# Sparse attention and an ELU layer on one core: more of the attention output transposed by DMA

## The chip, the cores and the metric

The kernel runs on one core of one Trainium2 chip. The metric is device time in microseconds (us) of one launch, lower is better. Three runs of the kernel before gave 321.51, 318.53 and 321.12 us, median 321.12.

## The reference

Eight batches of eight heads, 576 positions, 64 elements per head. Heads 0 to 3 are *local*: position i sees positions i-31 to i. Heads 4 to 7 are *strided*: i sees every earlier position with the same remainder modulo 32. Then an MLP with ELU over all 4608 tokens (512 to 2048 to 512).

```
rel = pos[:, None] - pos[None, :]
mask_local = (rel >= 0) & (rel < 32)
mask_strided = (rel >= 0) & (pos[None, :] % 32 == pos[:, None] % 32)
scores = where(mask, q @ k.T / sqrt(64), -1e9)          # per batch and head
attn = softmax(scores) @ v
x = attn.transpose(0, 2, 1, 3).reshape(8 * 576, 512)
h = x @ w_in
out = where(h > 0, h, exp(min(h, 0)) - 1) @ w_out
```

## The kernel before

**Tiles.** Two heads make a pair; a batch has two strided pairs S0, S1 and two local pairs L0, L1. A strided pair is cut into five groups of rows of like remainders, a local pair into six blocks of 96 queries. For each pair: transposed q and k (`qT`, `kT`), masked scores as probabilities `pr`, `av` (probabilities times v, with a column of ones for the sum), and `x`, the normalised result with tokens on the partitions. The MLP needs x with features on the partitions; that is `xT`, 128 features of a pair by all tokens, and making it is the step `x_out`.

**Order.** The instruction order is written by hand: there is no scheduler. After an opening for batch 0, nine stages run, one for each chunk of 512 tokens, nb = 0 to 8. Stage nb holds, in 16 steps s, the first MLP matrix of chunk nb (`moe_in`, four matmuls, L664), its ELU (`moe_act`: exp on ACT L690, then DVE L697 and L699) and the second matrix (`moe_out`, four matmuls, L713, mostly of chunk nb-1). Woven in between is the attention of batch nb+1: `attention` gives each piece of work a half step (a "gap", 0 to 31; gap 2s stands before `moe_in` of step s, gap 2s+1 behind it) from the table `TIMES`: where each pair begins, and the offsets of its pieces. In stages 1 and 2 the strided pairs come first, from stage 3 (batch `LATE` = 4) on the local ones. At about 31.5 us a stage, a gap is about 1 us.

**x_out.** For strided pairs, and for local pairs of batches 0 to 3, PE transposes the groups or blocks of `x` against an identity into PSUM (L607, L620), and ACT or DVE copies to `xT` (L614 and L616 put the strided rows in token order, L624 the local ones). Local pairs of batches 4 to 7 go by a DMA transpose that SP issues (L599), straight from `x` into `xT`.

**Loads and queues.** POOL issues all loads of a batch, strided q, k, v, then local q, k, v, three batches ahead (`load_batch`), each with a cast to bf16 into `nat`, which has three buffers for each of q and k. From batch 3 on, q and k are transposed by DMA (`transpose_batch`, issued on SP: L226 strided, one transfer each for q and k; L234 local, two each). SP also issues the stores of the result (L720). Each engine's queue runs in order: an instruction that waits holds back those behind it.

When `transpose_batch` was called before: for batch 3 at step 6 (strided) and 13 (local) of stage 1; for batch 4 at step 6 of stage 2, strided then local; for batches 5 to 7 at step 9 of stages 3 to 5, local then strided.

Of the kernel before, what the change touches and what calls it, by code (L numbers as in the profile page):

```python
# [14 lines left out]
ACT = mybir.ActivationFunctionType  # L15
# [14 lines left out]
C_ORDER = (2, 3, 0, 1)  # L30


PIECES = (-2, -1, 0, 2, 3, 5, 7, 0)
TIMES = (
    None,
    None,
    ((4, 10, 15, 21), 0, (-3, -2, 0, 2, 4, 6, 9, 2)),
    ((2, 9, 15, 22), 0, (-2, -1, 0, 2, 3, 5, 8, 0)),
    ((2, 8, 15, 22), 0, PIECES),
)  # L40


# [23 lines left out]
def kernel(  # L66
# [66 lines left out]
    def bf16_bank():  # L133
        return rings["ring"].next().bitcast(BF16)
# [17 lines left out]
    def several(n, name, *shape):  # L152
        return [consts.tile([128, *shape], BF16, tag=f"{name}{i}", name=f"{name}{i}")
                for i in range(n)]

    nat = {(n, kind): several(3, f"{n}_{kind}", w * D)
           for n in "qk" for kind, w in (("str", 20), ("loc", 4 * L_RUN))}

# [10 lines left out]
    BY_DMA = 3  # L171

    WHOLE = 2

    FAR = 1
    RAW = 1
# [42 lines left out]
                out=t[0:64, a, 4],  # L219
                in_=src[name][b, 2 * a:2 * a + 2, 512:576].rearrange("h p d -> p h d"))  # L220

    def transpose_batch(b, local):

        def strided():
            for name, to in (("q", qT), ("k", kT)):
                nc.sync.dma_start_transpose(out=to["str"][b % 2],  # L226
                                            in_=nat[name, "str"][b % 3])

        if BY_DMA <= b <= LATE and local < 2:
            strided()  # L230
        if b >= EARLY and local:
            for name, to, o in (("q", qT, 0), ("k", kT, 32)):
                for a in range(2):
                    nc.sync.dma_start_transpose(  # L234
                        out=to["loc"][b % 2][:, a, o:o + 640].rearrange(
                            "p (i r) -> p i r", r=128),
                        in_=nat[name, "loc"][b % 3][:, 640 * a:640 * a + 640])
        if b > LATE:
            strided()

    def load_batch(b):
        for name in "qkv":
# [20 lines left out]
    def clear_v(i, engine=nc.vector):  # L263
# [8 lines left out]
             for n in "q"}  # L272
# [2 lines left out]
    nc.scalar.activation(warm, ones[0:1, 0:1], ACT.Exp)  # L275
    nc.scalar.activation(rden.rearrange("p b s h r g -> p (b s h r g)"),
                         ones.to_broadcast([128, B * 48]), ACT.Copy)
    clear_nat(0)
    for i in range(2):
        nc.vector.memset(kT["str"][i][:, :, 126:128], 0.0)  # L280
# [70 lines left out]
    class Pair:  # L351
# [200 lines left out]
        def av(self, u):  # L552
            blocks = self.blocks(u)
            nk, nq = blocks[0][4:]
            b0 = blocks[0][1]
            n = len(blocks) // 2
            av = rings["ring"].next()[:, 0:6 * (D + 1)].rearrange(
                "q (p g d) -> q p g d", p=2, g=3)
            apart = self.strided and self.b == RAW
            vt = raw[RAW] if apart else (v_str if self.strided else v_loc)[self.b % 3]  # L560
            for p, blk, bank, i, _, _ in blocks:

                if self.b >= WHOLE:
# [5 lines left out]
                nc.tensor.matmul(to[:, 0:D] if apart else to, lhsT=pr[0:nk, o:o + m],  # L569
                                 rhs=vt[0:nk, 2 * self.hp + p, blk, :],  # L570
                                 start=True, stop=True)
# [13 lines left out]

        def step(self, what):
# [5 lines left out]
            else:  # L592
                getattr(self, {"x": "x_out"}.get(what, what))()

        def x_out(self):
# [7 lines left out]
            xt = bf16_bank()  # L603
            if self.strided:
                for g in range(5):
                    n = G_ROWS[g]
                    nc.tensor.transpose(  # L607
                        xt[:, 126 * g:126 * g + n],
                        self.x[0:n, g].rearrange("q p d -> q (p d)"),
                        identity[0:n, 0:n])  # L610
                rows = dst.rearrange("d (t r) -> d t r", r=STRIDE)
                groups = xt[:, 0:630].rearrange("d (g q) -> d g q", g=5)
# [22 lines left out]
    def attention(b, start, pitch, at):  # L635

        gaps = {}
        pairs = [Pair(b, s, hp) for s in (b < LATE, b >= LATE) for hp in range(2)]
        begin = [start + pitch * i for i in range(4)] if pitch else start
        if b >= LATE:  # L640
            gaps[begin[0]] = [pairs[3].halo]
        for i, pr in enumerate(pairs):
            for off, piece in ((at[0], pr.t_q), (at[1], pr.t_k),
                               (at[7], lambda pr=pr: pr.v_in(0)),
                               (at[7] + (b > 1), lambda pr=pr: pr.v_in(1)),
                               (at[2], lambda pr=pr: pr.scores(0)),
                               (at[3] if b < WHOLE else at[2] + (b < LATE),
                                lambda pr=pr: pr.scores(1)),
                               (at[4], lambda pr=pr: pr.av(0)),
                               (at[5] - (b >= LATE and i == 0),  # L650
                                lambda pr=pr: pr.av(1)),
                               (at[6] + (b > 1 and pr.strided) + (b >= LATE), pr.x_out), (at[5] - 2, pr.halo if b < LATE else lambda: None)):
                gaps.setdefault(begin[i] + off, []).append(piece)
        return gaps


# [145 lines left out]
    for nb in range(n_chunks + 1):  # L802
# [199 lines left out]
```

## Time and profile before

The profiled execution took 318.57 us, of which 316.8 are the span from the first to the last instruction. TensorE's granted clock was 0.996 in the mean.

| stretch | us | DVE busy | ACT busy | POOL busy | DMA share | PE instructions |
|---|---|---|---|---|---|---|
| chunk 1 (52.0 to 87.4) | 35.4 | 27.80 | 23.35 | 31.48 | 1.35 | 308 |
| chunk 2 (87.4 to 119.3) | 31.9 | 28.19 | 17.58 | 22.89 | 1.60 | 240 |
| chunk 3 (119.3 to 150.7) | 31.4 | 27.38 | 17.36 | 26.42 | 1.55 | 227 |
| chunk 4 (150.7 to 182.4) | 31.7 | 27.13 | 17.81 | 22.27 | 1.56 | 227 |
| chunk 5 (182.4 to 213.9) | 31.5 | 26.54 | 17.72 | 1.20 | 0.77 | 228 |
| chunk 6 (213.9 to 245.3) | 31.4 | 26.43 | 17.62 | 0.00 | 0.14 | 227 |

A row is one stage; the busy columns are us of each engine in it. A DMA share above 1 means that transfers overlap on the DMA engines. In the opening (to about 30 us) PE has gaps; from chunk 1 on it has next to none. How to read lines of the profile: L607 is line 607 of the kernel; PE is TensorE's matmul side, DVE is VectorE, ACT ScalarE, POOL GpSimd, SP SyncE, and a q behind a name (SPq) its queue, which issues DMAs. `single<-identity,x_s` is output <- inputs, and x5 the number of instructions merged into the line. The columns of a timeline are start, duration, engine, line, operation; a bracket gives the idle time before it and what ended that.

### The profile page before, as it was taken

The numbers are of one execution on the slowest core, as the hardware profiler recorded it, in microseconds if no ns is written. First come the engines' busy times: TensorE is split into PE (matmuls) and PEld (weight loads), VectorE is DVE, ScalarE is ACT, GpSimd is POOL, SyncE is SP. The second block draws the span as 40 slices with busy tenths as digits, with TensorE's granted clock in tenths as the row PEclk, the third lists the DMA queues.
The fourth block names the chain that finished last, engine by engine and source line by source line (L and its number), as shares of the span: only waits on it lengthen the run. The fifth ranks groups of instructions, "written<-read, shape, count | busy, mean of one in ns | idle before, by whom it ended". The sixth has DMA issues, their size and how long they took to land.

```text
span 316.8 us, 6114 instructions
## 1 busy us (share of the span) xinstructions
PE 299.8 (95%) x2240; PEld 149.1 (47%) x2240; DVE 242.6 (77%) x544; ACT 172.9 (55%) x335; POOL 137.5 (43%) x213
## 2 busy tenths in 40 slices
PE   1778989999999999999999999999999999999994
PEld 0454545545444554445444544454445444444443
DVE  7787797887889998987898788878897666766610
ACT  3577886777355645565546555655565444343411
POOL 9859526959959859958585810000000000000000
PEclk9999999999999999999999999999999999999998
DMA  6999999999999999999999992580210000101012
GB/s 108 163 179 157 167 207 126 156 124 183 139 125 167 157 187 138 99 163 154 177 163 117 163 175 61 88 156 35 68 35 35 34 33 35 66 34 36 33 68 73
DMA packets 108970, 36.33 MB, mean 115 GB/s; under 512 B 87357, under 2 KB 104453, under 8 KB 108933
## 3 DMA queue, kind: packets, MB, share of 16 engines
q0 software_dynamic: 71632, 18.10, 65.0%
q1 hardware_dynamic: 37301, 17.77, 29.1%
q8 instruction: 19, 0.31, 0.4%
q14 instruction: 18, 0.15, 0.1%
HBM read 36.70 MB, written 9.44 MB: 146 GB/s over the span
## 4 chain that ended last, share of the span: by engine, by line
PE 84%; DMA 6%; DVE 3%; POOL 2%; ACT 2%; issue 1%; POOLq 0%; ACTq 0%
PE single L713 39%; PE half L664 28%; PE single L664 9%; PE single L569 3%; DMA q_str<-in_q_dram 3%; PE pair_a L479 2%; DMA v_raw<-in_v_dram 2%; DMA k_str<-in_k_dram 2%; PE single L607 1%; ACT e_sb L690 1%; POOL k_str L191 1%; PE single L397 1%; DVE g_sb L699 1%; PE single L383 1%; DVE x_l L580 1%
## 5 line engine op out<-in xcount | busy, mean ns | idle before, releaser
L713 PE MATMUL single<-w_out_sb,g_sb 128*128 128x512 bf16 (+1 forms) x592 | 145.9, 373 | 0.0
L664 PE MATMUL half<-xT,w_in_sb 128*128 128x512 bf16 x436 | 112.6, 379 | 0.9 <-DVE g_sb L699 0.9
L690 ACT ACTIVATE e_sb<-half 128x512 f32<-128x512 f32 x109 | 65.3, 600 | 70.9 <-PE half L664 67.9
L697 DVE TENSOR_SCALAR e_sb<-e_sb 128x512 bf16<-128x512 f32 x140 | 62.5, 446 | 34.9 <-ACT e_sb L690 34.4
L713 PEld LDWEIGHTS <-g_sb 128*128 128x128 bf16 x592 | 54.8, 98 | 56.6
L664 PEld LDWEIGHTS <-w_in_sb 128*128 128x128 bf16 x576 | 52.4, 98 | 57.0 <-issue 1.3
L699 DVE TENSOR_TENSOR g_sb<-e_sb,half 128x512 bf16<-128x512 bf16 x106 | 72.9, 688 | 3.7
L664 PE MATMUL single<-xT,w_in_sb 128*128 128x512 bf16 x140 | 36.5, 379 | 0.0
L690 ACT ACTIVATE e_sb<-single 128x512 f32<-128x512 f32 x35 | 21.1, 602 | 24.4 <-PE single L664 22.3
L718 ACT COPY o_sb<-single 128x512 f32<-128x512 f32 (+1 forms) x37 | 21.2, 574 | 17.5 <-PE single L713 16.7
L485 ACT ACTIVATE pr<-pair_a 126x936 bf16<-126x936 f32 (+1 forms) x24 | 23.1, 961 | 12.4 <-PE single L479 11.9
L569 PEld LDWEIGHTS <-pr 128*128 128x128 bf16 (+3 forms) x352 | 20.0, 101 | 13.7 <-issue 1.3
L699 DVE TENSOR_TENSOR g_sb<-e_sb,single 128x512 bf16<-128x512 bf16 x34 | 23.4, 688 | 1.2
L191 POOL DMA_DIRECT2D k_str<-in_k_dram x32 | 21.1, 698 | 6.8 <-issue 2.6
L191 POOL DMA_DIRECT2D v_raw<-in_v_dram x32 | 20.7, 683 | 5.0 <-DVE v_str L436 3.7
L191 POOL DMA_DIRECT2D q_str<-in_q_dram x28 | 17.4, 641 | 4.1 <-DMA w_out_sb<-in_moe_w_out_dram 2.3
L580 DVE TENSOR_TENSOR x_l<-single,rden 96x384 bf16<-96x384 f32 x32 | 17.7, 554 | 1.1
L580 DVE TENSOR_TENSOR x_s<-single,rden 126x256 bf16<-126x256 f32 (+1 forms) x32 | 15.7, 491 | 1.1
L214 POOL DMA_DIRECT2D k_loc<-in_k_dram x20 | 15.3, 795 | 2.5 <-issue 1.5
L214 POOL DMA_DIRECT2D q_loc<-in_q_dram x20 | 15.8, 813 | 0.7 <-DMA k_str<-in_k_dram 0.7
L579 DVE RECIPROCAL rden<-single 96x6 f32<-96x6 f32 (+2 forms) x64 | 11.8, 185 | 2.0 <-PE single L569 1.6
L569 PE MATMUL single<-v_loc,pr 128*128 128x65 bf16 x192 | 11.6, 195 | 0.8 <-ACT v_loc L444 0.3
(115 smaller groups left out, 249.6 us busy)
## 6 DMA issues: line engine op xcount, KB each, us to landing
out_dram<-o_sb SPq DMA_DIRECT2D x35, 256.0 KB, 3.6
v_loc<-in_v_dram POOLq DMA_DIRECT2D x8, 288.0 KB, 8.2
k_str<-in_k_dram POOLq DMA_DIRECT2D x32, 67.5 KB, 5.0
v_raw<-in_v_dram POOLq DMA_DIRECT2D x32, 67.5 KB, 4.8
w_in_sb<-in_moe_w_in_dram POOLq DMA_DIRECT2D x4, 512.0 KB, 8.2
w_out_sb<-in_moe_w_out_dram POOLq DMA_DIRECT2D x4, 512.0 KB, 13.6
q_str<-in_q_dram POOLq DMA_DIRECT2D x28, 67.5 KB, 7.5
q_loc<-in_q_dram POOLq DMA_DIRECT2D x20, 64.0 KB, 5.2
```

The source lines that it names most:

```text
L191: engine.dma_start(out=t[0:108, h].rearrange("p g d -> p (g d)"), in_=rows[h, :, 0:30, :].rearrange("t (r g) d -> t r (g d)", g=5))
L214: nc.gpsimd.dma_start(out=t[:, h // 2, 0:4, h % 2], in_=src[name][b, h, 0:512].rearrange("(i p) d -> p i d", p=128))
L485: nc.scalar.activation(both, sc[0:nk, :, 0:w], ACT.Exp, scale=scale)
L569: nc.tensor.matmul(to[:, 0:D] if apart else to, lhsT=pr[0:nk, o:o + m], rhs=vt[0:nk, 2 * self.hp + p, blk, :], start=True, stop=True)
L579: nc.vector.reciprocal(r, av[0:nq, :, 0:n, D])
L580: nc.vector.tensor_tensor(self.x[0:nq, b0:b0 + n].rearrange("q g p d -> q p g d"), av[0:nq, :, 0:n, 0:D], r.unsqueeze(3).to_broadcast([nq, ...
L664: nc.tensor.matmul(hps, lhsT=w_in_sb[:, c, m * 128:(m + 1) * 128], rhs=xT[:, c, nb * N_TILE:(nb + 1) * N_TILE], start=start, stop=stop)
L690: nc.scalar.activation(e_sb, hps, ACT.Exp)
L697: nc.vector.tensor_scalar(e1_sb, e_sb, scalar1=1.0, scalar2=1.0, op0=ALU.min, op1=ALU.subtract)
L699: nc.vector.tensor_tensor(g_of[nb][:, m, :], e1_sb, hps, op=ALU.max)
L713: nc.tensor.matmul(ops, lhsT=g_of[nb][:, m, kk * 128:(kk + 1) * 128], rhs=w_out_sb[:, m, cols], start=(m == 0), stop=(m == MC - 1))
L718: nc.scalar.copy(o_sb, ops)
```

## The change

Strided `x` of batches 2 to 7 (the third to the last), and local `x` of the first pair of batches 2 and 3, no longer go through PE. `x_s` becomes two fixed buffers, one for each pair of a batch; ACT fills their last 32 partitions once at the start. A new piece `x_dma`, one gap after `av(1)`, has SP issue a DMA transpose of `x_s` into free space: the part of `nat["q", "str"]` of the same batch, whose q was already transposed. `x_out`, three gaps later than before (at most gap 31), copies from there to `xT` on ACT, by the same two copies. For the local pair SP issues the transpose straight into `xT`, as for later batches.

`transpose_batch` is split, and a table `TURNS` gives the steps: for batch 3 local 13, strided q and k 9; for batch 4 local 6, strided 8; for batches 5 to 7 local 8, strided q 11, strided k 14. In stages 3 to 6 the two strided pairs begin one and two gaps earlier.

With this the order on SP in stage 2 is: `x_s` of S0 (gap 8), a store, the four local transposes of batch 4 (step 6), `x_s` of S1 (gap 15), strided q and k of batch 4 (step 8), a store, `x_l` of L0 (gap 23). In stages 3 and 4: `x_l` of L0, the four local transposes, `x_l` of L1, a store, `x_s` of S0, strided q, a store, `x_s` of S1, strided k, a store.

```diff
+TURNS = ((13, 9, 9), (6, 8, 8), (8, 11, 14))
 TIMES = (
...
-    ((2, 8, 15, 22), 0, PIECES),
+    ((2, 8, 14, 20), 0, PIECES),
 )
...
+    x_str = several(2, "x_s", 6, 2, D)
...
+    X_DMA = 2
+    X_ONE = 2
+    X_WAIT = 3
...
-    def transpose_batch(b, local):
-
-        def strided():
-            for name, to in (("q", qT), ("k", kT)):
-                nc.sync.dma_start_transpose(out=to["str"][b % 2],
-                                            in_=nat[name, "str"][b % 3])
-
-        if BY_DMA <= b <= LATE and local < 2:
-            strided()
-        if b >= EARLY and local:
-            for name, to, o in (("q", qT, 0), ("k", kT, 32)):
...
-        if b > LATE:
-            strided()
+    def transpose_batch(b, s):
+
+        for what, at in zip(("loc", "str q", "str k"), TURNS[min(b - EARLY, 2)]):
+            if s != at:
+                continue
+            if what == "loc":
+                for name, to, o in (("q", qT, 0), ("k", kT, 32)):
...
+            else:
+                name = what[-1]
+                nc.sync.dma_start_transpose(out=(qT if name == "q" else kT)["str"][b % 2],
                                             in_=nat[name, "str"][b % 3])
...
+    for i in range(2):
+        nc.scalar.activation(x_str[i][96:128].rearrange("q g p d -> q (g p d)"),
+                             ones[96:128].to_broadcast([32, 12 * D]), ACT.Copy)
...
-            if self.x is None:
+            if self.strided:
+                self.x = x_str[self.hp]
+            elif self.x is None:
...
+        def by_dma(self):
+            if self.strided:
+                return self.b >= X_DMA
+            return self.b >= LATE or self.b >= X_ONE and self.hp == 0
+
+        def x_dma(self):
+            if self.strided and self.by_dma():
+                free = nat["q", "str"][self.b % 3][:, 640 * self.hp:640 * self.hp + 640]
+                self.x_t = free.rearrange("d (g q) -> d g q", g=5)
+                nc.sync.dma_start_transpose(
+                    out=self.x_t,
+                    in_=self.x[:, 0:5].rearrange("q g p d -> q (g p d)"))
+
         def x_out(self):
...
-            if self.b >= LATE and not self.strided:
+            if self.by_dma() and not self.strided:
...
+                if self.by_dma():
+                    groups = self.x_t
+                else:
...
+                               (at[5] + 1, pr.x_dma),
+                               (at[6] + (b > 1 and pr.strided) + (b >= LATE)
+                                + X_WAIT * (pr.strided and pr.by_dma()), pr.x_out), (at[5] - 2, pr.halo if b < LATE else lambda: None)):
+                gaps.setdefault(min(begin[i] + off, 31), []).append(piece)
...
-            if s == (9 if nb + 2 > LATE else 6) and nb > 0 and nb + 2 < B:
-                transpose_batch(nb + 2, int(nb + 2 >= LATE))
-            if s == 13 and nb + 2 == EARLY:
-                transpose_batch(nb + 2, 2)
+            if nb > 0 and nb + 2 < B:
+                if s in TURNS[min(nb + 2 - EARLY, 2)]:
+                    transpose_batch(nb + 2, s)
```

More of the change, by code (lines that the diff above doesn't have):

```diff
@@ L220, in load_local @@
                 in_=src[name][b, 2 * a:2 * a + 2, 512:576].rearrange("h p d -> p h d"))
-    def transpose_batch(b, local):
-        def strided():
-            for name, to in (("q", qT), ("k", kT)):
-                nc.sync.dma_start_transpose(out=to["str"][b % 2],
-                                            in_=nat[name, "str"][b % 3])
-        if BY_DMA <= b <= LATE and local < 2:
-            strided()
-        if b >= EARLY and local:
-            for name, to, o in (("q", qT, 0), ("k", kT, 32)):
[L233 to L237, printed above, removed]
-        if b > LATE:
-            strided()
+    def transpose_batch(b, s):
[4 more added lines that the diff above has]
+                for name, to, o in (("q", qT, 0), ("k", kT, 32)):
+                    for a in range(2):
+                        nc.sync.dma_start_transpose(
+                            out=to["loc"][b % 2][:, a, o:o + 640].rearrange(
+                                "p (i r) -> p i r", r=128),
+                            in_=nat[name, "loc"][b % 3][:, 640 * a:640 * a + 640])
+            else:
+                name = what[-1]
+                nc.sync.dma_start_transpose(out=(qT if name == "q" else kT)["str"][b % 2],
+                                            in_=nat[name, "str"][b % 3])
     def load_batch(b):
@@ L593, in step @@
                 getattr(self, {"x": "x_out"}.get(what, what))()
+        def by_dma(self):
[6 more added lines that the diff above has]
+                self.x_t = free.rearrange("d (g q) -> d g q", g=5)
+                nc.sync.dma_start_transpose(
+                    out=self.x_t,
+                    in_=self.x[:, 0:5].rearrange("q g p d -> q (g p d)"))
         def x_out(self):
@@ L602, in x_out @@
                 return
-            xt = bf16_bank()
+            if not self.by_dma():
+                xt = bf16_bank()
             if self.strided:
[L605 to L610, printed above, removed]
-                rows = dst.rearrange("d (t r) -> d t r", r=STRIDE)
-                groups = xt[:, 0:630].rearrange("d (g q) -> d g q", g=5)
+                rows = dst.rearrange("d (t r) -> d t r", r=STRIDE)
+                if self.by_dma():
+                    groups = self.x_t
+                else:
+                    for g in range(5):
+                        n = G_ROWS[g]
+                        nc.tensor.transpose(
+                            xt[:, 126 * g:126 * g + n],
+                            self.x[0:n, g].rearrange("q p d -> q (p d)"),
+                            identity[0:n, 0:n])
+                    groups = xt[:, 0:630].rearrange("d (g q) -> d g q", g=5)
                 copy = self.copy("x", False)
@@ L651, in attention @@
                                 lambda pr=pr: pr.av(1)),
-                               (at[6] + (b > 1 and pr.strided) + (b >= LATE), pr.x_out), (at[5] - 2, pr.halo if b < LATE else lambda: None)):
-                gaps.setdefault(begin[i] + off, []).append(piece)
+                               (at[5] + 1, pr.x_dma),
+                               (at[6] + (b > 1 and pr.strided) + (b >= LATE)
+                                + X_WAIT * (pr.strided and pr.by_dma()), pr.x_out), (at[5] - 2, pr.halo if b < LATE else lambda: None)):
+                gaps.setdefault(min(begin[i] + off, 31), []).append(piece)
         return gaps
```

## The prediction

> **What bounds the kernel now.** I read the page's busy lines first, then the waits of TensorE, then the timelines of PE, SP, POOL and ACT around every x transpose, then the landing times of the DMA transposes. The page's summary (busy time of each engine; DMA share in 40 slices of 7.9 us):
>
> ```profile
> PE 299.8 (95%) x2240; PEld 149.1 (47%) x2240; DVE 242.6 (77%) x544; ACT 172.9 (55%) x335; POOL 137.5 (43%) x213
> DMA  6999999999999999999999992580210000101012
> ```
>
> PE is busy nearly all the span, and its waits between 54 and 300 us come out as an empty list. So in chunks 1 to 8 each us taken off PE is a us gained, as long as nothing makes PE wait. The DMA engines are at nine tenths or more until 190 us: the loads of later batches fill them.
>
> The second half of chunk 2 (nb = 2, 87.3 to 119.3 us) decides my forecast. First PE there (start us, us, instruction), then SP's queue, then POOL's loads of batch 4:
>
> ```profile
> 105.20 0.42 PE L607 MATMUL single<-identity,x_s 126*128 126x126 bf16 x5
> 105.46 0.35 PE L569 MATMUL single<-v_loc,pr 128*128 128x65 bf16 x6
> ...
> 109.39 0.39 PE L479 MATMUL pair_a<-qT_loc,kT_loc 64*128 64x96 bf16 x10
> ...
> 112.61 0.35 PE L569 MATMUL single<-v_loc,pr 128*128 128x65 bf16 x6
> ```
>
> ```profile
> 98.61 3.11 SPq L226 DMA_TRANSPOSE qT_str<-q_str  x1
> 101.94 2.44 SPq L226 DMA_TRANSPOSE kT_str<-k_str  x1
> ...
> 106.56 2.59 SPq L234 DMA_TRANSPOSE qT_loc<-q_loc  x2
> 110.26 2.58 SPq L234 DMA_TRANSPOSE kT_loc<-k_loc  x2
> ```
>
> ```profile
> 104.73 0.63 POOL L218 DMA_DIRECT2D k_loc<-in_k_dram  x1
> 106.26 0.60 POOL L218 DMA_DIRECT2D k_loc<-in_k_dram  x1 [0.90 <-DMA q_loc<-in_q_dram]
> ```
>
> The reader is to see two things. Five x transposes hold PE for 0.26 us (105.20 to 105.46). And SP's local transposes of batch 4, asked for at step 6 (about 99 us), start at 106.56 and 110.26, because their loads are the last of the batch: SP waits 2.0 us for q_loc and 1.0 us for k_loc, and the two last k_loc loads land 5.4 and 4.3 us after their issue, at 110.1 and 110.6.
>
> The last view is the landing of the x_l transposes that are there already (min, median, max over eight; 5.6 at 162 us among loads, 2.6 at 225 us with none):
>
> ```profile
> DMA to landing us min/median/max: 2.6/4.1/5.6
> ```
>
> **The change, part by part. Removed from PE:** strided x of batches 2 to 7, 12 groups of five transposes. In every one the next instruction starts 0.25 to 0.26 us after the group: 12 x 0.257 = 3.1 us. The first local pair of batches 2 and 3 goes too, two groups of six (79.27 to 79.52, 110.62 to 110.88): 0.5 us. Together 3.6 us, all on the path. With them go two copies on DVE (0.45 us each, L624), which nobody waits for.
>
> **Kept on ACT:** the copies that interleave the strided rows (L614 0.61 us, L616 0.20 us), now from SBUF. A row for a copy of that kind is L444 on ACT, SBUF to SBUF, 640 elements in 0.72 us, 1.13 ns an element against 1.12 for L614: no change. At the start ACT fills two x_s buffers, 768 elements each; L276 takes 0.50 us for 384, so 0.5 to 1.0 us each. They lie in the 3.30 us in which ACT waits for q_stage (2.65 to 5.96); without that cover they cost up to 2.0.
>
> **Added to SP:** 14 DMA transposes, 1.2 us of SP each by the rows of L599 and L234 (1.20 to 1.28). SP works in order, so each stands behind what comes before it, and ACT's copy now waits for its landing, with everything on ACT behind it: the exps of the MoE (L690) and of the next scores (L485), hence DVE's maxima and PE.
>
> **Room between issue and copy:** six half steps of about 1 us in chunks 1 and 2, six and five later. Chunk 1: x_s of pair S1 is ready at 72.0 (L580 at 71.42); SP, with only an out store ahead, can issue then. The row nearest in time is the qT_str transpose at 69.6, landing 5.7 us later: 77.7, and ACT's copy is due at half step 23, about 78. The first local pair goes to SP behind qT_str and kT_str, about 79.5, and is needed at about 87.5; kT_loc took 9.1 us there. I put 0.3 us on chunk 1, between 0 and 1.5.
>
> **Chunk 2, the main cost.** For batch 4 the local transposes now come first, at step 6, the x transpose of S1 of batch 3 stands behind them (half step 15), then qT_str and kT_str. S1's x_s is ready at 103.4 (L580 at 102.81), but SP sits in front of k_loc. Loads share the DMA engines with the transposes: until 97 us three x transposes come on top, after 98 two strided ones go away; I take the loads 1 us earlier than before, uncertain by 2. Then the second kT_loc issues at 110.6, x_s1 at 111.8, and lands 4.1 us later, at 115.9. (From both sides: 2.6 after 110.8 is 113.4; 6.9, as the kT_loc of 110.26 took, after 112.85 is 119.8.) ACT's copy is due at half step 21, about 108.4. PE goes on through the scores of L1 and two more w_in groups, then needs L1's probabilities at the row 112.61, which the shortened program reaches 1.5 us sooner, at 111.1. These come after ACT's copies (0.8), exp (0.97) and DVE's mask (0.65, L487): 2.5 us after landing with the handovers. So PE stands from 111.1 to 118.4: **7.3 us**, between 4.8 and 11.2. Then the x of L0 of batch 3 waits in SP for x_s1, qT_str (3.1) and kT_str (2.4): issue near 119, landing 123 to 126; chunk 3 now starts near 124.8, so this hides behind the first stall, and would be the next one late without it.
>
> **PE after a stall.** In the opening PE idles 3.39 us until 6.41; then five transposes take 1.01 us, later sets 0.69 to 0.85, and only from 19 us on is 0.42 the rule. PE after 7 us of idling may thus run slow at first, though the clock row shows 1.00 throughout. 0 to 2 us, I take 1.0. [...]
>
> **Chunks 3 and 4.** With the strided pairs one and two half steps earlier, S1's x is ready near 145.3 in old time; SP has to finish qT_str (3.1), then the out store of step 12 (its o_sb copy ends at 145.9), and issues near 146.4. It lands 4.1 to 6.8 us later, 150.5 to 153.2. The next chunk's first group reads it (fourth matmul, 151.4) after 0.8 us of copies: PE waits 0 to 2.6 us in each of the two chunks that still have loads beside them. I take 1.0 and 0.5. In chunks 5 and 6 transposes land in 2.6 to 4.1 us: nothing. [...]
>
> **Hidden:** the load of q_str for batch b+3 now waits for batch b's copies, with POOL's queue behind it. Copies end at about 78, 109 to 117 and 151 to 158; POOL reaches these loads at 108.2, 131.8 and 158.5. Only the last is close.
>
> **Sum:** 318.57 - 3.6 + 0.3 + 7.3 + 1.0 + 1.5 = 325.1 us against the profiled execution (span 316.8 and 1.8 around it). That one is the low end of the runs shown (318.53 to 321.51, median 321.12), so for a median I go 1 us up: 326.
>
> **Rivals.** *No new waits.* If the local loads are in by the time SP asks, or ACT's blocked copy stays covered, 3.6 us come off: 315.0, with 0 to 2.6 for where the runs lie. For it: PE waits for nothing now, and ACT is busy 55%. Against it: SP did wait for q_loc until 106.56 although it asked later than it will. 0.15.
>
> *A stall that cancels the gain.* Loads 2 us earlier or more and landing in 2.6 us: x_s1 lands at 113.4 or before, PE loses at most 4.8, with no slow start and nothing at the chunk ends: 315.0 + 4.8 = 319.8. This ends not slower; it decides from a landing of 113.4. 0.27.
>
> *The chunk ends rule.* Chunk 2 passes freely, but x_s1 is late at the ends of chunks 3 to 6: 4 x 2.6 - 3.6 = +6.8, 325.4. Against it: landing 2.6 at 225 us. 0.05.
>
> My forecast: 0.53; its own range is 321.5 to 331.
>
> **How the numbers follow.** About 1% (3.2 us) is what a measurement of this kernel can tell from no change. More than 1% faster is only the first rival, and only if almost nothing is given back: 0.15. Within 1%: 0.30, the second rival and the light end of the forecast. Slower: 0.55. The range takes in the first rival's 315 and the forecast's upper bounds, 331.
>
> **What would show it.** Right: SP's kT_loc of batch 4 near 109 to 111, the x_s transpose right behind it, ACT waiting 5 to 9 us for that DMA before L643, PE idle once before the av of L1 in chunk 2, few us elsewhere. Wrong: the local transposes issuing near 99, or PE without waits in chunk 2 although ACT waits.

## The result, and the profile after

Six runs of the changed kernel gave 332.52 to 342.35 us, median 337.55; six of the kernel before, on the same chip, 318.53 to 321.60, median 320.79. The ratio is 1.045, with a 95% interval of 1.037 to 1.053: slower, in the direction of the forecast and well beyond its 326 and its range. The profiled execution took 335.6 us, 17.0 more than the profiled one of before; its span is 333.8 and TensorE's mean granted clock 0.977 (before 0.996). Here and below, medians and ranges are of all runs of a kernel and ratios of those within 1.5% of its fastest, and the profiles of three experiments (the late batches alone, the old order in chunk 2, one strided pair on TensorE) are of runs slower than that.

The page's busy times, and rows of its 40 slices (8.3 us each):

```profile
PE 299.2 (90%) x2129; PEld 146.9 (44%) x2168; DVE 244.1 (73%) x542; ACT 180.0 (54%) x337; POOL 136.7 (41%) x213
...
PE   1879989999999449999899959998999999999994
...
PEclk9999999999999959999999978999999999999999
DMA  6999999999999999989979990556052200011012
```

The weight loads of TensorE are 72 fewer (2240 before), the 72 transposes that were moved. But TensorE is no longer busy throughout: there are two slices at 4 and one at 5 in the middle, and the clock row has dips beside or behind them. TensorE's waits from 54 to 340 us, by what ended them (total, times, longest); before, this list was empty:

```profile
PE single L579 <- DVE pr L497: 8.9, 1, 8.9
PE half L695 <- ACT xT L645: 4.8, 3, 3.0
PE single L695 <- ACT xT L645: 0.8, 1, 0.8
PE single L579 <- DVE v_str L446: 0.7, 1, 0.7
```

With small ones these are 16.4 us. The first is chunk 2. SP's timeline there, then ACT's, then PE's (start, duration, engine, line, operation; in the bracket the idle time before and its releaser):

```profile
104.81 2.60 SPq L239 DMA_TRANSPOSE qT_loc<-q_loc  x2
109.10 2.65 SPq L239 DMA_TRANSPOSE kT_loc<-k_loc  x2
111.85 1.60 SPq L616 DMA_TRANSPOSE q_str<-x_s  x1
113.50 2.96 SPq L245 DMA_TRANSPOSE qT_str<-q_str  x1
116.52 2.03 SPq L245 DMA_TRANSPOSE kT_str<-k_str  x1
...
119.27 1.31 SPq L624 DMA_TRANSPOSE xT<-x_l  x1
```

```profile
118.17 1.10 ACT L643 COPY xT<-q_str 128x540 bf16<-128x540 bf16 x1 [9.35 <-DMA q_str<-x_s]
119.17 0.22 ACT L645 COPY xT<-q_str 128x36 bf16<-128x36 bf16 x1
119.30 0.96 ACT L495 ACTIVATE pr<-pair_a 128x960 bf16<-128x960 f32 x1
```

```profile
111.08 1.03 PE L695 MATMUL half<-xT,w_in_sb 128*128 128x512 bf16 x4
121.01 0.52 PE L579 MATMUL single<-v_loc,pr 128*128 128x65 bf16 x6 [8.90 <-DVE pr L497]
121.33 1.90 PE L744 MATMUL single<-w_out_sb,g_sb 128*128 128x512 bf16 x4
123.02 1.53 PE L695 MATMUL half<-xT,w_in_sb 128*128 128x512 bf16 x4
...
124.58 1.03 PE L744 MATMUL single<-w_out_sb,g_sb 128*128 128x512 bf16 x3
```

The x transpose issues at 111.85, behind the local transposes, and lands just before 118.2, when ACT's copy can start; the exp of L1's scores stands behind that copy, and the probabilities come to PE at 121.0. After the wait four matmuls of 512 columns take 1.90 and 1.53 us, where 1.03 is the rule. The landing of the x transposes (min, median, max, from issue):

```profile
DMA to landing us min/median/max: 2.6/5.0/7.8
```

This view has the landing of only four of the twelve. The trace also records the counts of the semaphores (the counters that tell an engine that a transfer is done), sixteen for each DMA; the last of the sixteen gives the landing of all: 4.5 to 7.8 us for the eight that land while a load is under way, 2.6 to 4.2 for the four behind the last load. In chunk 2 it is 118.07, 6.2 us after the issue.

The length of each stage, from the first copy of a result tile in it (L749 on ACT, L718 before) to that in the next stage, in us:

| stage | before | after | difference | the prediction's terms |
|---|---|---|---|---|
| 1 | 35.00 | 35.57 | +0.57 | -0.5 |
| 2 | 31.96 | 41.94 | +9.98 | +7.5 |
| 3 | 31.45 | 32.49 | +1.04 | +0.5 |
| 4 | 31.67 | 35.31 | +3.64 | 0.0 |
| 5 | 31.45 | 33.70 | +2.25 | -0.5 |
| 6 | 31.46 | 31.42 | -0.04 | -0.5 |

The last column sums the prediction's gains (0.26 for five transposes, ten a stage, six more in stages 1 and 2) and losses for each stage. It foresaw where the largest loss is; it is 11 us short in all, and 6 of those lie in stages 4 and 5, at the end of chunk 4 and behind it.

### The profile page after: what moved, and what is told of

Read it like the earlier page. It is cut to its first block, busy times and chain, and to the rows that moved or that the text cites. A ratio compares the mean times of both kernels' runs of the same rounds, so it can differ in the third digit from the quotient of the medians.

```text
span 333.8 us, 5988 instructions
## 1 busy us (share of the span) xinstructions
PE 299.2 (90%) x2129; PEld 146.9 (44%) x2168; DVE 244.1 (73%) x542; ACT 180.0 (54%) x337; POOL 136.7 (41%) x213
## 4 chain that ended last, share of the span: by engine, by line
PE 59%; DMA 19%; POOL 8%; issue 5%; ACT 3%; DVE 3%; SPq 1%; ACTq 0%; POOLq 0%; DVEq 0%
PE single L744 28%; PE half L695 18%; PE single L695 8%; DMA q_str<-x_s 6%; DMA w_out_sb<-in_moe_w_out_dram 5%; DMA k_str<-in_k_dram 3%; DMA v_loc<-in_v_dram 3%; PE single L579 2%; PE pair_a L489 2%; DMA v_raw<-in_v_dram 2%; POOL v_raw L200 1%; DVE g_sb L730 1%; POOL k_str L200 1%; DMA k_loc<-in_k_dram 1%; DVE e_sb L728 1%
## 5 line engine op out<-in xcount | busy, mean ns | idle before, releaser
L728 DVE TENSOR_SCALAR e_sb<-e_sb 128x512 bf16<-128x512 f32 x140 | 64.7, 462 | 43.0 <-ACT e_sb L721 42.3
L744 PEld LDWEIGHTS <-g_sb 128*128 128x128 bf16 x592 | 55.6, 99 | 64.3 <-issue 9.2
L695 PEld LDWEIGHTS <-w_in_sb 128*128 128x128 bf16 x576 | 53.3, 99 | 60.3 <-issue 2.9
L749 ACT COPY o_sb<-single 128x512 f32<-128x512 f32 (+1 forms) x37 | 21.3, 574 | 20.4 <-PE single L744 20.0
L200 POOL DMA_DIRECT2D v_raw<-in_v_dram x32 | 20.6, 690 | 18.4 <-DVE v_str L446 17.1
L200 POOL DMA_DIRECT2D k_str<-in_k_dram x32 | 20.2, 663 | 6.0 <-issue 2.9
L643 ACT COPY xT<-q_str 128x540 bf16<-128x540 bf16 x12 | 13.4, 1119 | 15.8 <-DMA q_str<-x_s 13.4
L579 PE MATMUL single<-v_loc,pr 128*128 128x65 bf16 x192 | 11.9, 197 | 10.4 <-DVE pr L497 8.9
L592 DVE TENSOR_TENSOR x_l<-single,rden 96x384 bf16<-96x384 f32 x32 | 17.7, 554 | 1.1
L497 DVE TENSOR_TENSOR pr<-pr,mask_l 128x960 bf16<-128x960 bf16 x12 | 7.9, 656 | 11.9 <-ACT pr L495 11.7
L592 DVE TENSOR_TENSOR x_s<-single,rden 126x256 bf16<-126x256 f32 (+1 forms) x32 | 15.7, 491 | 1.1
```

Of the source, the lines that this page charges most:

```text
L200: engine.dma_start(out=t[0:108, h].rearrange("p g d -> p (g d)"), in_=rows[h, :, 0:30, :].rearrange("t (r g) d -> t r (g d)", g=5))
L592: nc.vector.tensor_tensor(self.x[0:nq, b0:b0 + n].rearrange("q g p d -> q p g d"), av[0:nq, :, 0:n, 0:D], r.unsqueeze(3).to_broadcast([nq, ...
L695: nc.tensor.matmul(hps, lhsT=w_in_sb[:, c, m * 128:(m + 1) * 128], rhs=xT[:, c, nb * N_TILE:(nb + 1) * N_TILE], start=start, stop=stop)
L728: nc.vector.tensor_scalar(e1_sb, e_sb, scalar1=1.0, scalar2=1.0, op0=ALU.min, op1=ALU.subtract)
L744: nc.tensor.matmul(ops, lhsT=g_of[nb][:, m, kk * 128:(kk + 1) * 128], rhs=w_out_sb[:, m, cols], start=(m == 0), stop=(m == MC - 1))
L749: nc.scalar.copy(o_sb, ops)
```

## The experiments

The theories, as they stood at the start. A: the place of the x transposes in SP's queue in chunk 2 makes the large stall, and the rest follows. B: the waits at chunk ends come from their own places in the queue. C: ACT's copy from SBUF, 1.12 us where the one from PSUM takes 0.61, is what costs. D: a transpose of x takes longer to land beside loads than there is room before its copy. E: ACT, standing in front of a copy whose x has not landed, holds back the exps behind it. F: the one local pair of batch 3 makes the runs scatter. D, E and F came with the results. Ratios are to the kernel before on the same chip, with 95% intervals. All edits are against the changed kernel; where a text says "on top of" another experiment, that one's edit belongs to it too.

**x ahead of the local transposes.**

```diff
-TURNS = ((13, 9, 9), (6, 8, 8), (8, 11, 14))
+TURNS = ((13, 9, 9), (8, 9, 9), (8, 11, 14))
```

> Batch 4's local transposes are asked for at step 8 instead of 6 and its strided ones at step 9, so that SP meets the x transpose of batch 3's second strided pair ahead of them; nothing else differs from the changed kernel. Theory A (the place in SP's queue makes the 8.9 us stall of TensorE in chunk 2, and the slow matmuls after it, the late loads of batches 6 and 7 and the later waits at chunk ends follow from it): the x transpose issues near 104.5 us and lands by 111, TensorE's wait for L1's probabilities falls from 8.9 to under 2, POOL's waits for the v_str copy from 17.1 to about 4, chunk-end waits from 5.6 to about 2; 322 to 326 us. Theory B (the chunk-end waits are made by their own places in the queue): the 8.9 goes, the 5.6 at the chunk ends stay; 328 to 330. Theory C (the ACT copy from SBUF, 1.12 us where the one from PSUM took 0.61, is what costs): 334 or more.

340.22 us, 1.061 [1.050, 1.071]. The transpose issued at 107.07 and landed 3.35 us later, TensorE's wait for L1's probabilities fell from 8.9 to 0.5, and the time did not fall: the start of chunk 3 now waited for the local pair's x, whose transpose SP issued at 122.72, after the local and the strided ones of batch 4. PE there:

```profile
122.52 0.59 PE L695 MATMUL single<-xT,w_in_sb 128*128 128x512 bf16 x2
129.69 1.01 PE L695 MATMUL single<-xT,w_in_sb 128*128 128x512 bf16 x2 [6.58 <-DMA xT<-x_l]
130.50 1.91 PE L744 MATMUL single<-w_out_sb,g_sb 128*128 128x512 bf16 x4
```

So the queue's order does make the first stall, and A's sum fell all the same: SP holds two x transposes among eight of the next batch, and moving one ahead leaves the other late. The waits at the chunk ends stayed (1.85, 2.95, 1.05, 0.32), as B says. The number is in C's range (334 or more), but the 6.6 us have another cause.

**The late batches alone.**

```diff
-    X_DMA = 2
+    X_DMA = 4
-    X_ONE = 2
+    X_ONE = 4
```

> Batches 2 and 3 have all their x transposed on TensorE again (four groups of five and two of six, about 1.6 us of TensorE back); batches 4 to 7 keep their strided x by DMA, and the order of SP's other transposes is that of the changed kernel. Theory A: no stall in chunk 2, the loads in time again, chunk-end waits 1 to 2 us; 322 to 326 us. Theory B: chunk-end waits of 5 us remain: 326 to 330. If the DMA transposes were free at the chunk ends: 318 to 320.

327.21 us (323.79 to 328.80), 1.016 [1.008, 1.023]. The median lies in B's range, but two of the four runs, 323.79 and 325.71, lie in A's, so the times do not decide. The waits do: the chunk ends hold 6.5 us in the profile, where A expected 1 to 2. Chunk 2 is quiet, and batches 4 to 7 alone cost 5 us by the ratio. SP, ACT and PE at the end of chunk 3 of this kernel:

```profile
145.27 3.51 SPq L245 DMA_TRANSPOSE qT_str<-q_str  x1
149.12 0.34 SPq L751 DMA_DIRECT2D out_dram<-o_sb  x1
149.56 1.25 SPq L616 DMA_TRANSPOSE q_str<-x_s  x1
```

```profile
156.05 1.10 ACT L643 COPY xT<-q_str 128x540 bf16<-128x540 bf16 x1 [2.62 <-DMA q_str<-x_s]
157.05 0.22 ACT L645 COPY xT<-q_str 128x36 bf16<-128x36 bf16 x1
```

```profile
157.32 0.40 PE L695 MATMUL half<-xT,w_in_sb 128*128 128x512 bf16 x1 [2.54 <-ACT xT L645]
157.53 1.89 PE L744 MATMUL single<-w_out_sb,g_sb 128*128 128x512 bf16 x4
```

x was ready at 148.4 (DVE's L592), waited 1.1 us for SP, took 6.4 to land, and TensorE waited for the copies. At the ends of chunks 4 to 6 it waited 2.46, 0.32 and 1.14.

**No strided x by DMA, but the rest of the change.**

```diff
-    X_DMA = 2
+    X_DMA = 8
-    X_ONE = 2
+    X_ONE = 4
```

> No strided x by DMA, and the local pairs of batches 2 and 3 on TensorE as before the change: what is left of the change is the order of SP's transposes, the strided pairs of batches 4 to 7 one and two half steps earlier, and the two x buffers filled at the start. Theories A to C: these cost nothing by themselves, the time is that of the kernel before, within 1 us (320 to 322). Rival: the reordering delays batch 4's strided q and k, or the fills the start; then 323 or more, and TensorE shows a new wait between 54 and 320 us or starts later.

319.80 us, 1.000 [0.998, 1.002]: the new order of SP's transposes, the earlier strided pairs and the two fills cost nothing.

**The copy in another order.**

```diff
-copy(rows[:, :, 0:30].rearrange("d t (r g) -> d t r g", g=5),
-     groups[:, :, 0:108].rearrange("d g (t r) -> d t r g", r=6))
+copy(rows[:, :, 0:30].rearrange("d t (r g) -> d g t r", g=5),
+     groups[:, :, 0:108].rearrange("d g (t r) -> d g t r", r=6))
```

> The larger ACT copy of strided x walks its source in order (six neighbouring elements innermost, written five apart) instead of reading 128 elements apart and writing in order; the values are the same. If the 1.12 us come from reading SBUF with a long stride, the copy takes 0.6 to 0.75 us; if from SBUF as such or from the interleaved writing, 1.1 or more. Theory A: only the copies that TensorE waits behind count, five times 0.4 us: 335 to 337 us. Theory C (ACT's extra 6 us are the loss): 331 to 332.

343.76 us (339.70 to 347.07), above both ranges, and the copy got longer, 1.80 us from SBUF and 1.76 from PSUM: not the 0.6 to 0.75 expected if reading with a long stride is the cause, though the new order writes 10 bytes apart, so this does not clear the long read. It serves as a rough test of C all the same. Four copies lie in the opening, where the first `moe_out` came at 51.93 us after 44.38; from there to the end it took 287.7 us, and 289.4 in the profile of the changed kernel. So 8 us more of ACT's time in the stages (twelve copies, 0.68 each) cost nothing that shows in these two profiles. The test is rough because the stall in chunk 2 happened to be shorter, 4.98 us, x having landed in 4.7. What speaks against C as the main cause is a later run: without loads the eight copies of 1.12 us are still there and the time is 0.999.

**The old order in chunk 2:** strided transposes of batch 4 at step 6, x of S1, local ones at step 8.

```diff
-TURNS = ((13, 9, 9), (6, 8, 8), (8, 11, 14))
+TURNS = ((13, 9, 9), (8, 6, 6), (8, 11, 14))
```

> The whole change, but in chunk 2 SP takes batch 4's strided transposes at step 6 and its local ones at step 8, so that both the x transpose of batch 3's second strided pair and the one of its first local pair have nothing late in front of them (the run that put only the local ones back lost 6.6 us on the local pair's transpose, which stood behind the strided ones). Theory A (the queue order of chunk 2 makes the stall): no wait over 1 us in chunk 2; what is left over the kernel before are the chunk-end waits of the run with the late batches alone (6.4 us), less the transposes off TensorE in batches 2 and 3 (1.6 us): 324 to 327 us. If the x transposes of batches 2 and 3 cost for another reason (loads beside them, TensorE's clock): 330 or more.

330.41 us, 1.031 [1.025, 1.036] against 1.045: about a third of the loss is back, not what A expected. In the profile, taken at 338.65, waits of 3.34 us (probabilities of L1) and 1.91 (local x) are left, with x ready at 104.3, issued at 105.76 behind the strided k, and landing at 113.4, 7.6 us later.

**One strided pair of the late batches on TensorE**, on top of the old order.

```diff
-            return self.b >= X_DMA
+            return self.b >= X_DMA and not (self.b >= LATE and self.hp)
```

> As the run before it, and the second strided pair of batches 4 to 7 has its x transposed on TensorE; eight groups of five and two of six stay off TensorE (2.6 us). Theory B (only the last pair's transpose is late at a chunk end: about 6 us from issue to landing beside loads, and a copy of 1.34 us before the next chunk's first group): the chunk-end waits vanish, and the time is 316 to 320 us, under the kernel before. If the first pair's transpose or the ACT copies behind it are late as well: 321 or more, with ACT's wait for that transpose ahead of a wait of TensorE.

324.96 us (321.13 to 326.74), 1.012 [1.006, 1.017]. No wait at the chunk ends for the last copy any more, but the first pair's is late too, in the middle of the stage. ACT and PE:

```profile
148.16 0.59 ACT L749 COPY o_sb<-single 128x512 f32<-128x512 f32 x1 [0.48 <-PE single L744]
153.62 1.10 ACT L643 COPY xT<-q_str 128x540 bf16<-128x540 bf16 x1 [4.88 <-DMA q_str<-x_s]
154.63 0.22 ACT L645 COPY xT<-q_str 128x36 bf16<-128x36 bf16 x1
154.76 0.59 ACT L721 ACTIVATE e_sb<-half 128x512 f32<-128x512 f32 x1
```

```profile
156.58 1.02 PE L695 MATMUL half<-xT,w_in_sb 128*128 128x512 bf16 x4 [3.01 <-DVE g_sb L730]
```

Nothing needs that x yet. ACT stands in front of its copy, an MLP exp stands behind it, DVE's `g_sb` behind that, and TensorE waits 3.01 us for DVE to be done with `half`. This is E.

**Strided q behind x**, on the late batches alone.

```diff
-TURNS = ((13, 9, 9), (6, 8, 8), (8, 11, 14))
+TURNS = ((13, 9, 9), (6, 8, 8), (8, 14, 14))
```

> As the run with the late batches alone, but from batch 5 on the strided q transpose is asked for at step 14 instead of 11, behind the x transpose of the second strided pair (which follows it at once in the queue, and 3.5 us of SP's time less stand ahead of it). If q's transpose ahead of x is what makes x late: x lands within 4.5 us of issue, chunk-end waits fall from 6.4 to under 3, 321 to 324 us. If the loads beside it do (they are there in chunks 3 and 4 only), or the fixed path from x ready to the copy: waits of 2 us or more remain at the ends of chunks 3 and 4; 325 to 328 us.

323.98 us, 1.010 [1.005, 1.016]; the interval overlaps that of the late batches alone, so the gain is not shown by the times. The second pair's x still took 6.0 and 4.7 us to land in chunks 3 and 4, not the 4.5 expected if the strided q ahead of it were what makes it late. In the profile the wait for the last copy went in chunk 3 and fell to 1.34 in chunk 4, and one of 2.67 for `g_sb` came in chunk 3: the wait moved from the second pair's x to the first's, for which ACT stood 4.27 us.

**Without the q and k loads of batches 6 and 7**, on the late batches alone.

```diff
-        for name in "qkv":
+        for name in "qkv" if b < 6 else "v":
             load_strided(b, name)
-        for name in "qkv":
+        for name in "qkv" if b < 6 else "v":
             load_local(b, name)
```

> The kernel with the late batches alone, without the loads of q and k of batches 6 and 7 (their attention computes on older data, so the output differs there); they are the loads that stand beside the x transposes of chunks 3 and 4. Theory D (a transpose of x takes 6 to 7 us to land beside loads and 2.6 to 4 without, and the room left for it is 4 to 5): the x transposes of batches 4 and 5 land within 4.5 us, TensorE's waits of 2.5 us at the ends of chunks 3 and 4 fall under 0.8 each, 319 to 323 us. Theory B (the place in SP's queue): the two waits stay at 2 us or more, 325 to 328 us.

322.68 us, 1.006 [1.002, 1.009]. The second pair's x landed in 3.0 and 4.2 us, and the waits of 2.5 fell to 1.1 and 1.0, now for `g_sb`: x of the first pair still landed late, at 150.0 and 182.8, after issues at 142.56 and 174.63. POOL's last load before each of them:

```profile
140.49 1.45 POOL L211 DMA_DIRECT2D v_loc<-in_v_dram  x1
173.79 1.21 POOL L211 DMA_DIRECT2D v_loc<-in_v_dram  x1 [0.41 <-issue]
```

They landed 9.4 and 9.0 us after issue, at 149.9 and 182.8: the same moments, within 0.2 us. Hence the next run.

**Without any load of batches 6 and 7.**

```diff
+        if b > 5:
+            raw[b] = raw[b - 2]
+            return
```

> The kernel with the late batches alone, without any load of batches 6 and 7, the v loads included (their attention computes on older data). In the run without q and k, x of the first strided pair still landed 7.6 and 8.2 us after issue, at the moment that the load of v_loc landed. Theory D: with the v loads gone too it lands within 4 us, no wait of TensorE over 0.6 us in chunks 3 and 4; 318 to 321 us. Theory B: ScalarE still waits 2.6 us for x of the first strided pair in both chunks, 322 to 323 us as in that run.

319.53 us, 0.999 [0.995, 1.002]: Theory D. The x transposes of this kernel, landing (min, median, max of two; by the semaphore counts seven of the eight landed in 2.6 to 2.9 us, the last in 4.2):

```profile
DMA to landing us min/median/max: 2.6/2.6/2.6
```

ACT waited for none of them in chunks 3 and 4, and TensorE 0.32 us at each end. SP's queue was the same; what is gone is the loads. So B, which expected ACT to wait 2.6 us as before, falls for these chunks.

**Copies on GpSimd**, with the old order in chunk 2 and strided q behind x.

```diff
-TURNS = ((13, 9, 9), (6, 8, 8), (8, 11, 14))
+TURNS = ((13, 9, 9), (8, 6, 6), (8, 14, 14))
-copy = self.copy("x", False)
+copy = nc.gpsimd.tensor_copy if self.by_dma() else self.copy("x", False)
```

> The whole change with SP's transposes in the best order so far (batch 4: strided at step 6, local at 8; from batch 5 on both strided ones at step 14, behind the last x), and the copies of strided x that came by DMA made by GpSimd instead of ScalarE. Theory E (ScalarE, standing in front of a copy whose x has not landed, holds back the exps and so TensorE): no wait of TensorE for probabilities or for DVE's g_sb over 0.5 us; what is left is the wait for x itself at the ends of chunks 3 and 4, 1 to 3 us each; 322 to 327 us. Rival: GpSimd needs 3 us or more for a copy, or its wait holds back the loads behind it; then 329 or more.

351.23 us, 1.095 [1.091, 1.100]: the rival, by another way. A copy takes 1.12 us there too, but GpSimd's queue is full of loads: the copies of x whose transposes were issued from 64.4 us on began at 108.9, and TensorE waited 23.65 us for them. It says nothing on E.

**The same order, copies on ACT** (of the diff above, the line of `TURNS` alone).

> The same order of SP's transposes, with the copies on ScalarE. If the gains of the two reorderings add (330.4 for the old order of chunk 2, and the 3.2 us that q behind x brought the late batches): 326 to 329 us, with waits over 1 us in chunk 2 and 3 where ScalarE waits for x. If one of them takes back the other's: 330 or more. Set beside the run with GpSimd's copies it gives the price of ScalarE's waiting: Theory E 3 us or more, otherwise under 1.

328.48 us (324.77 to 328.68), 1.026 [1.023, 1.029], at the upper end. The profiled run is the one at 324.77: waits of 1.60, 2.04, 1.70 and 0.74 us, and a clock of 0.999.

**Room.** Old order in chunk 2, last pair on TensorE, local and strided q transposes at steps 11 and 12 from batch 5 on, and copies three half steps later.

```diff
-TURNS = ((13, 9, 9), (6, 8, 8), (8, 11, 14))
+TURNS = ((13, 9, 9), (8, 6, 6), (11, 12, 14))
-    X_WAIT = 3
+    X_WAIT = 6
-            return self.b >= X_DMA
+            return self.b >= X_DMA and not (self.b >= LATE and self.hp)
```

> Strided x by DMA for batches 2 and 3 whole and for the first strided pair of batches 4 to 7 (the second on TensorE), and more room between issue and copy: three half steps more for each copy, batch 4's strided transposes at step 6 and local ones at step 8, from batch 5 on local and strided q transposes at steps 11 and 12, so that the x transpose of the first strided pair has no transpose of a load in front of it at step 10. Theory D (x lands 6 to 8 us after its issue beside loads; ScalarE standing at the copy is what reaches TensorE): with 8 to 9 us of room TensorE has no wait over 1 us, and the 2.6 us of transposes that stay off it (eight groups of five, two of six) show: 317 to 319 us. If the added DMA traffic costs elsewhere (loads later, local transposes at step 11 late for the next chunk): 321 or more.

The profiled run, 318.84 us, has what D and E expect: ACT waits for no x, and TensorE's longest wait is one of 0.78, for the local pair's x at the start of chunk 3. Stages 5 and 6 took 31.19 and 31.20 us where the kernel before took 31.45 and 31.46: 0.26 for five transposes, as the prediction had it. Stage 2 took 32.77, 0.81 more than before. But twelve runs lie from 318.11 to 326.79, median 322.88, six of them at 323.19 or above; the ratio is 0.998 [0.993, 1.003].

**The local pair of batch 3 on TensorE as well.**

```diff
-self.b >= X_ONE and self.hp == 0
+self.b == X_ONE and self.hp == 0
```

> The kernel with room, and the first local pair of batch 3 transposed on TensorE again (0.27 us back). In the profile of the kernel with room its x was ready at 108.9 us, stood in SP behind the local transposes until 115.0 and landed 0.8 us late for chunk 3, the only wait there; half of that kernel's runs were 4 to 8 us longer than the profiled one. Theory F (where the loads of batch 4 come a little later, this x is later by as much, and TensorE's clock halves after the wait): without it the runs lie together, 317 to 320 us, median about 319. Rival: the spread comes from x of the strided pairs or from loads made later by the added transposes: half the runs stay above 322.

Twelve runs from 317.46 to 321.18, median 319.43, 0.999 [0.996, 1.001]. The spread is gone with that one transpose, as F expected. How it makes a run late is not shown: no run of the kernel with room above 318.84 was profiled, and the two kernels ran on different chips. The 2.3 us that TensorE no longer spends are not seen in the time, and the interval has no room for them. In the profile stages 3, 5 and 6 are 0.25 to 0.27 us shorter than before, but stages 1, 2 and 4 are 0.12 to 0.42 longer; what takes the gain back there was not followed.

**DMA only where it is quiet:** batch 2, and the first strided pair of batches 6 and 7, with the old order in chunk 2.

```diff
-            return self.b >= X_DMA
+            return self.b == X_DMA or self.b >= 6 and self.hp == 0
-self.b >= X_ONE and self.hp == 0
+self.b == X_ONE and self.hp == 0
```

> Strided x by DMA only where little stands beside it: batch 2 whole, and the first strided pair of batches 6 and 7; the first local pair of batch 2 by DMA; all other x on TensorE as before the change. Four groups of five and one of six stay off TensorE: 1.3 us. Theory D: no wait of TensorE over 0.5 us after the opening, 318 to 319.5 us, runs lie together. If DMA transposes of x cost even without loads beside them: 320.5 or more.

318.89 us (317.31 to 322.87), 0.998 [0.995, 1.001], with no wait of TensorE over 0.6 us after the opening. Two of the twelve runs, at 322.44 and 322.87, lie apart. No version was shown to beat the kernel before; the 1.3 us that this one should gain are within what the interval leaves open.

## Why the prediction was wrong: the direction right, the sum too small

**Off TensorE, 3.6 us: right.** 0.26 us for five, in stages without a wait. **Fills, order and earlier pairs at nothing: right** (1.000 without the DMAs). **Chunk 1, 0.3:** the profile has 1.0 us of waits there (0.65 for `v_str`, 0.38 for `x_l`), inside its bounds, but by luck: the prediction feared a late x, and the run without strided x by DMA has such waits too (0.53 and 0.26).

**Chunk 2, 7.3 us: the mechanism right, the size 1.6 short.** Issue at 111.85 where 111.8 was predicted; PE stood from 112.1 to 121.0, 8.9 us. The term that failed is the landing: 4.1 us taken, 6.2 measured. (The way from there to PE took 2.9 us, not 2.5, and PE ran dry 1.0 later.) The prediction took 4.1 for the median of eight `x_l` transposes, but its view had the landing of only two of them, one among loads and one with none. The semaphore counts of the kernel before give all eight: 4.9, 7.9, 5.7 and 5.3 us beside loads, 2.5 to 2.6 for the four behind them. The nearest row, kT_loc at 110.26 with 6.9, had been put down as the upper end.

**The local pair's x "hides behind the first stall, and would be the next one late without it": right.** The first experiment shows it, with 6.58 us.

**Chunk ends, 1.0 and 0.5, and nothing in chunks 5 and 6: this step failed.** TensorE waited 1.40, 3.04, 0.83 and 0.32 us, 5.6 in all. The path was seen (SP free, landing, two copies, first group of the next chunk), but two links were taken too short. At the end of chunk 4:

```profile
188.34 0.34 SPq L751 DMA_DIRECT2D out_dram<-o_sb  x1
188.77 1.26 SPq L616 DMA_TRANSPOSE q_str<-x_s  x1
```

```profile
195.29 1.09 ACT L643 COPY xT<-q_str 128x540 bf16<-128x540 bf16 x1 [2.64 <-DMA q_str<-x_s]
196.29 0.22 ACT L645 COPY xT<-q_str 128x36 bf16<-128x36 bf16 x1
```

```profile
196.56 0.59 PE L695 MATMUL half<-xT,w_in_sb 128*128 128x512 bf16 x1 [3.04 <-ACT xT L645]
```

x landed 6.4 us after issue, the two copies took 1.2 instead of 0.8, and PE had run dry 4.8 us after the issue. At the ends of chunks 3, 5 and 6 the landing was 4.8, 4.2 and 2.6 us. In chunks 5 and 6, with no load beside x, that is about what the prediction took (2.6 to 4.1), and TensorE waited 0.83 and 0.32 all the same; with copies of 0.8 us it would have been 0.4 and nothing, an estimate. The copy was priced by L444, 1.13 ns an element; it took 1.12 us for 540 elements, 2.07 ns each, 0.51 us longer than from PSUM. L444 reads and writes 64 neighbouring elements at a time, L643 reads single ones 256 bytes apart; the copy that writes 10 bytes apart took 1.80 us. No run separates the stride from other differences of these copies.

**PE after a stall, 1.0 once: this step failed too.** The clock was 0.50 for 3.0 us after chunk 2's stall (1.5 us lost) and for 6.0 us, of which PE worked 5.7, after the one of 3.04 at 196.56 (2.8 lost), a stall that the prediction took for at most 2.6 us and gave no slow clock. Together the terms of the profile come to -3.6 + 16.4 + 4.3 = 17.1; the measured difference is 17.0.

**The blocked ACT queue.** The prediction had it in chunk 2 alone. In stages 3 and 4 ACT stood at the first pair's copy too, 0.56 and 1.28 us in the changed kernel, where TensorE did not feel it; in the runs with one pair, with q behind x and without the q and k loads it did (3.01, 2.67 and 1.11 us). At the chunk ends the prediction asked only when x is needed, not when ACT would first stand in front of it.

**Rivals and range.** *No new waits* needed the local loads to be in when SP asks; kT_loc issued at 109.10, and PE stood 8.9 us. *A stall that cancels the gain* needed x at 113.4 or before; it came at 118.1. *The chunk ends rule* was given 0.05, and only with a chunk 2 that passes freely. The stall and the chunk ends came together: the late batches alone cost 5 us by the ratio, the whole change 14; that the early batches alone would cost the rest no run shows. The prediction's own bounds (11.2, 1.5, 2.0 and twice 2.6) led to 336 us for a median, and the range stopped at 331: the upper end of the forecast was not carried through.

**Open.** One run of each kernel was profiled, so why the times of one kernel scatter, over 8 us in the kernel with room, is not shown.

## What to carry to other kernels

A transpose moved from TensorE to a DMA was paid here mainly in latency: measure the landing beside the loads that run at that moment (4.5 to 7.8 us in the changed kernel, 2.6 to 4.2 without), and leave that much between issue and the first instruction, on any engine, that stands in front of it. An engine that copies what has landed and also feeds the critical path is held back by a late transfer long before anyone needs the data: with one pair on TensorE, ACT stood 4.88 us in front of a copy, and TensorE waited 3.01, while nothing needed that x yet. On a queue that runs in order, look for the second transfer behind the same obstacle before moving the first: with x ahead of the local transposes, TensorE waited 6.58 us for the other x.

## What the runs showed of the hardware

**The clock after short waits.** All waits of TensorE of 0.95 us or more in stages 1 and later, in the profiles of the changed kernel and of the fourteen experiments, and the granted clock in the microseconds after:

| wait, us | cases | clock at 0.50 afterwards |
|---|---|---|
| 0.96 to 1.91 | 16 | 0 |
| 2.04 to 2.67 | 11 | 6 |
| 2.95 to 23.65 | 9 | 9 |

Where it halved it stayed so for 2.9 to 6.4 us after the wait (10.4 where a second wait fell into the slow stretch). With half of that time counted as lost, a wait of about 3 us costs 4.7 to 6.1, an estimate. Every such slow stretch is 3.41 us long in the clock's records, or twice, three or eight times that; the two of the changed kernel after chunk 1 are of 6.83 us, from 117.20 and from 195.71. The clock halved after no wait of 1.91 us or less, after 6 of the 11 of 2.04 to 2.67 and after all 9 of 2.95 or more. In these runs, then, two microseconds of waiting were worth avoiding for themselves, and waits of like length cost differently; what decides among the 11 is not shown.

**Landing beside loads.** By the semaphore counts of all sixteen profiles, the 147 transposes of `x_s` and `x_l` that were in flight together with a load landed 2.6 to 10.2 us after issue, median 5.7; the 131 others took 2.5 to 4.5, median 2.6. Loads make the landing long as a rule and not always: the 3.35 us of the first experiment had loads beside them. In the run without q and k loads x of the first pair, issued at 142.56, landed at 150.0 with a v load issued 2 us before it by another engine; in the run without any load it took 2.9 us, though SP's queue was the same.
